# Bringing two kinds of short matmul bursts together in a Fourier and max-out kernel

## The chip, the cores and the metric

One core of a Trainium2 chip runs the whole program. The metric is device time in microseconds, the median of several executions. Less is better.

## The reference

```
X = np.fft.rfft(x, axis=1)                 # x: 8 batches of 3072 x 256
Yr = Xr @ w_r - Xi @ w_i + b_r
Yi = Xr @ w_i + Xi @ w_r + b_i
Y = soft_threshold(Yr, 0.01) + 1j * soft_threshold(Yi, 0.01)
y = np.fft.irfft(Y, n=3072, axis=1)        # then 24576 tokens of 256
h = max(y @ w1, y @ w2, y @ w3)            # 256 x 768 each
out = h @ w_out                            # 768 x 256
```

## The kernel before

**The Fourier part** of a batch is cut into stages. 3072 is 96 times 32. `stage_a` (L615) transforms over the 96 for one *quad*, four of the 32 columns, so a batch has eight quads i = 0 to 7. `stage_b` (L779) does the transform over the 32 for one of twelve groups k, `stage_w`, `stage_w1` and `stage_w2` multiply by the complex weights, `finish_w` (L905) splits the thresholded result *v* into a high and a low half-precision part, and `stage_q` (L934) is the first half of the inverse. `inverse` (L1077) is its second half. Between stages the data goes through device memory: a_d after stage a, z_d after stage q.

**Two of the stages use quarter-array matmuls.** From batch 3 on, `stage_a` multiplies 48 rows by 64 columns (L625), and `stage_q` for the middle groups multiplies *v* as 64 by 64 (L960). Each is a *burst* of 12 matmuls that run four at a time, three rounds of 512 columns, and fills two PSUM tiles. `stage_q` handles two groups in one burst, at k = 1, 3, 5, 7, 9, and group 10 alone in a burst of 256 columns. All other matmuls use the full array.

**The max-out part** is the main loop. It goes over batches b, eight chunks c of a batch and six slices f of the 768, 48 *slots* a batch. A slot has the first product of a new tile pu (six matmuls of 384 columns, `up` with i = 0, then a Relu in place on ScalarE), the second product of the tile before (`up` with i = 1, then h, on VectorE for every third f, else on ScalarE), and `down`, nine matmuls or more of 256 columns into pd. Everything is done in high and low halves, so each product is three matmuls (`mm3`, L184 to L186), and each result is split: ScalarE writes hi (hh, vb, xhl, tt), VectorE writes lo.

**The order around the change** is set by a list of events. `at(position, function, index)` puts a stage call at a position counted in slots, and `run_until` (L1006) runs what is due three times in a slot: after the first product, between the second product and `down`, and after `down`. So the Fourier work of batch b + 1 is threaded between the products of batch b, and stage a of batch b + 2 beside it. Group k of batch b has its base at `(b - 1) * SLOTS - 1.2 + 2.72 * (k + 2)` (L994), and its calls stand at offsets from it; quad i of batch b has its base at `(b - 2) * SLOTS + 5.6 * i` (L980).

**PSUM** has eight tiles of 512 columns. After the start, `ff_tile` gives tiles of one ring of three, "ff", to every Fourier stage (px, py, pi, pa, pz, pt). The ring "up" of three holds the pu tiles, and the ring "dn" of two holds pd. A new tile of a ring waits until the third tile before it (the second, in "dn") has been read for the last time. Both tiles of a stage-a burst come from "ff" before the change. Engines take their instructions strictly in the order written, so an instruction that waits holds up all that stand behind it on its engine.

Of the kernel before, what the change touches and what calls it, by code (L numbers as in the profile page):

```python
# [9 lines left out]
F32 = mybir.dt.float32  # L10
# [91 lines left out]
def fourier_maxout_kernel(  # L102
# [3 lines left out]
    NB, S, D = x.shape  # L106
    FF = w1.shape[1]
    P = 128
# [6 lines left out]
    NJP = 12  # L115
    SLOTS = NCH * NF
    NATIVE = 2 * NCH
    HALF_X = 3 * NCH
    SEVEN = {NB - 1: range(NF)}
    EARLY = NCH + 5  # L120
    FIRST = 32

    const = ctx.enter_context(tc.tile_pool(name="const", bufs=1))
# [3 lines left out]
    ps = ctx.enter_context(tc.tile_pool(name="ps", bufs=3, space=PSUM))  # L127
# [36 lines left out]
    def in_turn(turn=True):  # L164
        both = ExitStack()
        if turn and "slot" in st:
            for e in ("act", "dve"):
              if e in st:
                both.enter_context(tc.issue_after(st[e].ins))
        return both  # L170
# [12 lines left out]
    def mm3(o, lh, ll, rh, rl, start=True, stop=True, **kw):  # L183
        nc.tensor.matmul(o, lh, rh, start=start, stop=False, **kw)  # L184
        nc.tensor.matmul(o, lh, rl, start=False, stop=False, **kw)  # L185
        st["mm"] = nc.tensor.matmul(o, ll, rh, start=False, stop=stop, **kw)  # L186
# [4 lines left out]
    def ff_tile(name):  # L191
        tag = spare[0]
        if len(spare) > 1:
            spare.append(spare.pop(0))
        return ps.tile([P, 512], F32, name=name, tag=tag, bufs=2 if tag == "dn" else 3)
# [28 lines left out]
    def raw_tile(name):  # L224
        return ffn.tile([P, 1536], F32, name=name, tag="raw", bufs=8)

    def quad_tile(name):
        return fft.tile([P, NQ * D], F32, name=name, bufs=1 if name == "zq" else 2)[0:96]
# [259 lines left out]
    def at(pos, fn, i, k=None, n=None):  # L488
        if n is None or 0 <= k < n:
            events.append((pos, len(events), fn, i))  # L490

    def batch(b, kind):
        if (b, kind) not in st:
            if kind in "az":
                st[b, kind] = dram.tile([96, N2, D], F32, name=kind + "_d")
            else:
                w = 2 * NCH if kind == "x" else 2 * NJP
                st[b, kind] = fft.tile([P, w], F32, name="mx" + kind, bufs=3)
        return st[b, kind]
# [9 lines left out]
    def load_x(q):  # L509
        b, q4 = divmod(q, NCH)  # L510
        xv = x[b].rearrange("(n1 n2) d -> n1 n2 d", n2=N2)[:, q4 * NQ:(q4 + 1) * NQ, :]
        with tc.issue_after(st["ld"].ins) if q >= EARLY else nullcontext():
            if q == EARLY - 1:
                pairs = [fft.tile([P, 2, D], F32, name="xv", tag="vl", bufs=3)[0:N1] for _ in range(2)]
# [3 lines left out]
                return  # L518
            if 2 <= q < NCH or NCH + 2 <= q < EARLY:
                xq = raw_tile("xr")[0:N1, 0:NQ * D]  # L520
# [17 lines left out]
    def largest_x(q, i, xp):  # L538
        b, q4 = divmod(q, NCH)
        with tc.issue_after(quiet[0]) if q < EARLY else in_turn():  # L540
            nc.vector.tensor_reduce(
                out=batch(b, "x")[0:N1, 2 * q4 + i:2 * q4 + i + 1], in_=xp, axis=AX.X,
                op=ALU.max, apply_absolute_value=True,
            )
# [36 lines left out]
    def split_x(q):  # L581
# [12 lines left out]
        for i, xp in enumerate(pairs):  # L594
            if q >= EARLY:
                largest_x(q, i, xp)
# [11 lines left out]
    def store_a(q, r):  # L608
        b, q4 = divmod(q, NCH)
        nc.gpsimd.dma_start(  # L610
            out=batch(b, "a")[r, q4 * NQ:(q4 + 1) * NQ, :],
            in_=st["aq", q][r].rearrange("p (n d) -> p n d", n=NQ),
        )

    def stage_a(q):  # L615
        b, q4 = divmod(q, NCH)
        if q >= HALF_X:
            xt = st.pop(("xs", q))
            pa = [ff_tile("pa") for _ in range(2)]
            aq = fft.tile([P, NQ * D], F32, name="aq", bufs=2)  # L620
            for t, i in ((0, 0), (0, 1), (1, 0)):
                for r in range(2):
                    rows = slice(64 * r, 64 * r + 48)
                    for h in range(2):
                        st["mm"] = nc.tensor.matmul(  # L625
                            pa[r][64 * h:64 * h + 64], ft[rows, t], xt[rows, i, h],
                            start=t == i, stop=t == 1,
                        )
            av = batch(b, "a").rearrange("(k e c) n d -> e k c (n d)", e=2, c=2)
            for r in range(2):  # L630
                o = aq[:, 512 * r:512 * r + 512]
                nc.scalar.activation(out=o, in_=pa[r], func=AF.Copy, scale=1.0 / (X_SCALE * F_SCALE))  # L632
                for h in range(2):
                    n = q4 * NQ * D + h * 512
                    nc.gpsimd.dma_start(out=av[1 - r, :, :, n:n + 512], in_=o[64 * h:64 * h + 48])  # L635
            return
        st["aq", q] = aq = first_quads[q] if q < EARLY else quad_tile("aq")
        for i, xp in enumerate(st.pop(("xs", q))):
          with tc.issue_after(st["gate"]) if EARLY <= q < NATIVE else nullcontext():
            pa = ff_tile("pa")  # L640
            if q < NATIVE:
                nc.tensor.matmul(pa[0:96], fr, xp, start=True, stop=True)  # L642
            else:
                mm3(pa[0:96], fh, fl, *xp)
            nc.scalar.activation(
                out=aq[:, i * 512:i * 512 + 512], in_=pa[0:96], func=AF.Copy
            )
        if NCH <= q < EARLY:
            behind_z.append((q4, aq))
            return  # L650
        store_a(q, slice(0, 96 if b else FIRST))
        if NCH <= q < HALF_X and q4 == NCH - 1:
            scale_x(b, 2 * NCH)

    def scale_x(b, n, and_then=None):
        low, add = st["lim", "x"]

        def scales(e):
            st[b, "sx"] = power("s0x", e, -1.0, 261.0), power("s1x", e, 1.0, add)
            m = small("mv", bufs=2)  # L660
            nc.vector.tensor_scalar(
                out=m, in0=e, scalar1=add, scalar2=st["eb"], op0=ALU.add, op1=ALU.max
            )
            nc.vector.tensor_scalar(out=m, in0=m, scalar1=230.0, scalar2=None, op0=ALU.min)
            st[b, "sv"] = power("s0v", m, -1.0, 231.0), power("s1v", m, 1.0, 11.0)
            nc.vector.tensor_scalar(
                out=st[b, "sv"][1], in0=st[b, "sv"][1], scalar1=-1.0, scalar2=None, op0=ALU.mult
            )
            if and_then:
                and_then()  # L670

        exponent_of(st.pop((b, "x"))[0:N1, 0:n], "x", 23, 0xFF, low, scales)
# [261 lines left out]
    def stage_q(k):  # L934
# [35 lines left out]
        if kb == NJP - 1:  # L970
# [4 lines left out]

            exponent_of(st.pop((b, "u")), "u", 23, 0xFF, low, scales)

    for q in range(EARLY, NB * NCH):
        b, i = divmod(q, NCH)
        p = i if b == 1 else 9 + 5.2 * i if b == 2 else (b - 2) * SLOTS + 5.6 * i  # L980
        at(p - (3 if b == 1 else 5 if b == 2 else 8), load_x, q)
        if q >= HALF_X:
            at(p - 1, sum_x, q)
        at(p - 0.4 * (q >= HALF_X), split_x, q)
        at(p + 1, stage_a, q)
        if q >= HALF_X:
            p = 9 + 5 * i if b == 3 else (b - 3) * SLOTS + 5.5 * i + 5
            at(p - 4, load_m, q)
            at(p, largest_m, q)
            if i == NCH - 1:  # L990
                at(p + 1, scale_m, b)
    for b in range(1, NB):
        for k in range(-2, NJP + 1):
            p = 8 + 2.13 * (k + 2) if b == 1 else (b - 1) * SLOTS - (1.2 if b > 2 else 0.4) + 2.72 * (k + 2)  # L994
            for d, fn, i in (
                (0, load_a, k + 3), (-2.2 if b > 2 else -1.6, split_a, k + 1), (1.6, finish_w, k - 1),
                (1, stage_b, k + 1), (4 if k < NJP else 3, stage_q, k - 1), (2, stage_w, k), (2.4, stage_w2, k),
            ):
                at(p + d, fn, b * NJP + i, i, NJP)
            if k == -2:  # L1000
                at(p - (2.5 if b > 2 else 0), load_a, b * NJP)
# [292 lines left out]
    def idle_matmuls(n):  # L1294
        p = ff_tile("idle")
        for _ in range(n):
            nc.tensor.matmul(p, zeros[:, 0:P], zeros, start=True, stop=True)
# [8 lines left out]
    for q in range(NCH):  # L1306
        split_x(q)
        stage_a(q)
    for q in range(NCH):
        store_a(q, slice(FIRST, 96))  # L1310
    idle_matmuls(26)
# [89 lines left out]
    for q in range(NCH, EARLY):  # L1401
        split_x(q)
        if q < EARLY - 1:
            stage_a(q)
# [127 lines left out]
```

## Time and profile before

| | us |
|---|---|
| median of 3 runs | 1742.68 (1740.84 to 1744.57) |
| the profiled execution's own time | 1737.65 |
| its span, first to last instruction | 1735.9 |
| TensorE matmul busy | 1713.4, 99% of the span |
| VectorE busy | 1269.0, 73% |
| ScalarE busy | 1169.1, 67% |
| GpSimd busy | 292.2, 17% |
| granted TensorE clock | full speed in all 40 slices of the span |

Matmul durations in the trace overlap, since a matmul starts before the one ahead of it has ended. What one costs in a stream is read from the distance between starts.

### The profile page before, as it was taken

Reading aid. Unit: us, or ns where it says so; the run is one execution under the profiler, and the core shown is the slowest. Engines: PE = TensorE matmul, PEld = TensorE weight load, DVE = VectorE, ACT = ScalarE, POOL = GpSimd, SP = SyncE. Lnnn points to the kernel's source line nnn. Section 1 sums busy time; section 2 is a strip of 40 time slices with the busy share of each in tenths; the row PEclk is TensorE's granted clock in tenths of the full one; section 3 lists DMA queues with packets and bytes.
Section 4 is the critical chain, followed back from the end, with each engine's and each line's share of the span. In section 5 each row is a group of like instructions: output and inputs, shape, how many; then the busy total and the mean of one; then the engine's idle time right before and its main releaser. Section 6 shows DMA issues by size and latency. Waiting matters only on the chain.

```text
span 1735.9 us, 42087 instructions
## 1 busy us (share of the span) xinstructions
PE 1713.4 (99%) x16171; PEld 1278.0 (74%) x16171; DVE 1269.0 (73%) x2690; ACT 1169.1 (67%) x2493; POOL 292.2 (17%) x523
## 2 busy tenths in 40 slices
PE   8999999999999999999999999999999999999998
PEld 5866777677776777777777777777777777778998
DVE  2887887687866788678876688757787467667775
ACT  4567676677766777667775777667776566666775
POOL 2101012111221212211221111211222110110000
PEclk9999999999999999999999999999999999999999
DMA  9866565577646767466766567555753443422121
GB/s 294 249 183 195 161 167 162 159 183 190 186 120 178 181 185 192 133 175 177 191 168 167 156 178 204 159 143 153 191 160 106 121 126 104 122 78 64 56 60 34
DMA packets 203863, 269.61 MB, mean 155 GB/s; under 512 B 31438, under 2 KB 153262, under 8 KB 203566
## 3 DMA queue, kind: packets, MB, share of 16 engines
q1 hardware_dynamic: 171294, 193.34, 42.4%
q0 software_dynamic: 24736, 66.62, 12.0%
q10 hardware_dynamic: 7632, 6.95, 1.4%
q8 instruction: 128, 2.10, 0.5%
q14 instruction: 73, 0.60, 0.1%
HBM read 124.31 MB, written 75.50 MB: 115 GB/s over the span
## 4 chain that ended last, share of the span: by engine, by line
PE 81%; DVE 9%; DMA 5%; ACT 4%; issue 1%; SPq 1%; ACTq 0%; POOL 0%; DVEq 0%; POOLq 0%
PE pu L184 11%; PE pu L186 11%; PE pu L185 11%; PE pd L184 8%; PE pd L186 8%; PE pd L185 8%; PE py L184 3%; PE py L186 3%; PE py L185 3%; PE pi L1091 2%; PE px L792 2%; PE pa L625 2%; PE pz L960 2%; PE pu L1176 2%; PE pa L642 1%
## 5 line engine op out<-in xcount | busy, mean ns | idle before, releaser
L184 PE MATMUL pu<-yh,wuh 128*128 128x384 f16 x1344 | 438.6, 326 | 0.0
L186 PE MATMUL pu<-yh,wul 128*128 128x384 f16 x1344 | 438.0, 326 | 0.0
L185 PE MATMUL pu<-yl,wuh 128*128 128x384 f16 x1344 | 438.0, 326 | 0.0
L184 PE MATMUL pd<-woh,hh 128*128 128x256 f16 x1152 | 314.1, 273 | 0.6 <-ACT o L1273 0.4
L186 PE MATMUL pd<-woh,hh 128*128 128x256 f16 x1152 | 313.8, 273 | 0.1
L185 PE MATMUL pd<-wol,hh 128*128 128x256 f16 x1152 | 313.8, 273 | 0.0
L176 DVE TENSOR_TENSOR hh<-h,hh 128x384 f16<-128x384 f32 x336 | 185.9, 553 | 110.2 <-ACT hh L175 109.9
L1142 ACT ACTIVATE pu<-pu 128x384 f32<-128x384 f32 x336 | 160.7, 478 | 145.1 <-PE pu L186 135.1
L175 ACT ACTIVATE hh<-h 128x384 f16<-128x384 f32 x336 | 174.4, 519 | 70.2 <-DVE h L1146 64.9
L186 PEld LDWEIGHTS <-wul 128*128 128x128 f16 x1344 | 131.4, 98 | 86.7
L635 POOL DMA_DIRECT2D a_d<-aq x160 | 94.9, 597 | 584.9 <-ACT aq L632 573.5
L184 PEld LDWEIGHTS <-wuh 128*128 128x128 f16 x1344 | 131.3, 98 | 83.3 <-issue 21.6
L1278 POOL DMA_DIRECT2D out_dram<-o x189 | 104.5, 559 | 449.2 <-ACT o L1273 446.0
L185 PEld LDWEIGHTS <-wuh 128*128 128x128 f16 x1344 | 131.4, 98 | 62.5 <-issue 1.0
L1150 ACT ACTIVATE h<-pu 128x384 f32<-128x384 f32 x226 | 109.4, 484 | 47.1 <-PE pu L186 42.7
L184 PE MATMUL py<-wch,tt 128*128 128x256 f16 x504 | 137.4, 273 | 0.6 <-ACT aq L632 0.3
L186 PE MATMUL py<-wch,tt 128*128 128x256 f16 x504 | 137.3, 273 | 0.0
L185 PE MATMUL py<-wcl,tt 128*128 128x256 f16 x504 | 137.3, 272 | 0.0
L184 PEld LDWEIGHTS <-hh 128*128 128x128 f16 x1152 | 112.6, 98 | 33.0 <-issue 11.8
L185 PEld LDWEIGHTS <-hh 128*128 128x128 f16 x1152 | 112.7, 98 | 21.5 <-issue 0.5
L1105 DVE SCALAR_TENSOR_TENSOR y<-pi,ye 128x192 f32<-128x192 f32 x252 | 110.4, 507 | 21.8 <-ACT ye L1099 21.6
L186 PEld LDWEIGHTS <-hh 128*128 128x128 f16 x1152 | 112.6, 98 | 13.8 <-DVE hh L176 0.4
(288 smaller groups left out, 3551.0 us busy)
## 6 DMA issues: line engine op xcount, KB each, us to landing
zq<-z_d SPq DMA_DIRECT2D x63, 384.0 KB, 4.7
out_dram<-o POOLq DMA_DIRECT2D x189, 128.0 KB, 3.5
ab<-a_d SPq DMA_DIRECT2D x84, 256.0 KB, 4.3
ab<-ab SPq DMA_DIRECT2D x336, 64.0 KB, 2.8
vb<-vb SPq DMA_DIRECT2D x308, 64.0 KB, 2.9
z_d<-zs POOLq DMA_DIRECT2D x70, 256.0 KB, 3.9
xm<-in_x_dram SPq DMA_DIRECT2D x40, 384.0 KB, 4.3
a_d<-aq POOLq DMA_DIRECT2D x160, 96.0 KB, 3.3
```

What stands on the lines that cost most here:

```text
L175: nc.scalar.activation(out=hi, in_=src, func=AF.Copy)
L176: later(lambda: nc.vector.tensor_tensor(out=lo, in0=src, in1=h, op=ALU.subtract))
L184: nc.tensor.matmul(o, lh, rh, start=start, stop=False, **kw)
L185: nc.tensor.matmul(o, lh, rl, start=False, stop=False, **kw)
L186: st["mm"] = nc.tensor.matmul(o, ll, rh, start=False, stop=stop, **kw)
L625: st["mm"] = nc.tensor.matmul(pa[r][64 * h:64 * h + 64], ft[rows, t], xt[rows, i, h], start=t == i, stop=t == 1,)
L635: nc.gpsimd.dma_start(out=av[1 - r, :, :, n:n + 512], in_=o[64 * h:64 * h + 48])
L792: nc.tensor.matmul(pv[:, h, :, g // 2, g % 2], ah[:, g // 2, g % 2, h * P:(h + 1) * P], mb_sb[:, i, 4 * kb + g].rearrange("p (c m) -> p c ...
L1105: nc.vector.scalar_tensor_tensor(out=yv[:, e], in0=pv[:, 0], scalar=(1 - 2 * e) * Y_SCALE, in1=ev, op0=ALU.mult, op1=ALU.add,)
L1142: st["act"] = nc.scalar.activation(out=p, in_=p, func=AF.Relu)
L1150: st["act"] = nc.scalar.activation(out=h32, in_=p, func=AF.Relu, scale=H_SCALE)
L1278: nc.gpsimd.dma_start(out=out_v[b, c, t + i], in_=o[:, i])
```

## The change

A function `pace` holds the base of group k; for batches 3 and later it is 1.2 slots sooner than before (-2.4 in place of -1.2). With PAIR = 6.12, `stage_q` for the even k of batches 2 to 6 (those are the two-group bursts) moves from base + 4 to base + 6.12. Quads 3 to 7 of batches 3 to 7 are put at the same position, ahead of it in the list, with their loads, sums and splits 1 slot and more before. The second tile of every stage-a burst comes from the ring "up".

```diff
+    PAIR = 6.12
...
-            pa = [ff_tile("pa") for _ in range(2)]
+            pa = [ff_tile("pa"), ps.tile([P, 512], F32, name="pa", tag="up", bufs=3)]
...
+    def pace(b, k):
+        return 8 + 2.13 * (k + 2) if b == 1 else (b - 1) * SLOTS - (2.4 if b > 2 else 0.4) + 2.72 * (k + 2)
+
     for q in range(EARLY, NB * NCH):
         b, i = divmod(q, NCH)
-        p = i if b == 1 else 9 + 5.2 * i if b == 2 else (b - 2) * SLOTS + 5.6 * i
+        p = i if b == 1 else 9 + 5.2 * i if b == 2 else (b - 2) * SLOTS + 5.6 * i if i < 3 else pace(b - 1, 2 * i - 4) + PAIR - 1
...
-        at(p + 1, stage_a, q)
+        at(pace(b - 1, 2 * i - 4) + PAIR if b > 2 and i > 2 else p + 1, stage_a, q)
...
-            p = 8 + 2.13 * (k + 2) if b == 1 else (b - 1) * SLOTS - (1.2 if b > 2 else 0.4) + 2.72 * (k + 2)
+            p = pace(b, k)
...
-                (1, stage_b, k + 1), (4 if k < NJP else 3, stage_q, k - 1), (2, stage_w, k), (2.4, stage_w2, k),
+                (1, stage_b, k + 1), (PAIR if 1 < b < NB - 1 and k % 2 == 0 and k < NJP - 1 else 4 if k < NJP else 3, stage_q, k - 1), (2, stage_w, k), (2.4, stage_w2, k),
```

Line numbers after the change are higher by 1 to 4. In the rows below a number behind a tile's name tells its buffers apart.

First place: TensorE in batch 3 of the main loop, where stage a's burst for quad 4 ends. Before:

```order
L625 LDWEIGHTS zeros_72
L625 MATMUL pa_12363<-xhl_12268,zeros_72 64x512
L184 LDWEIGHTS wuh_81
L184 MATMUL pu_12385<-yh_12110,wuh_81 128x384
L185 LDWEIGHTS wuh_81
```

After:

```order
L626 LDWEIGHTS zeros_72
L626 MATMUL pa_12546<-xhl_12450,zeros_72 64x512
L961 LDWEIGHTS zeros_72
L961 MATMUL pz_12566<-vb_12002,zeros_72 64x512
L961 LDWEIGHTS zeros_72
```

The burst of stage a was followed by a full-array product; now the burst of stage q follows it with nothing between. There are 25 such places, five in each of the main loop's batches 1 to 5.

Second place: ScalarE around the last pair of batch 3 of the main loop. h32 and hh are h and its high part, aq and zs are what is read out of pa and pz. Before, around the same product of *v* (group 9):

```order
L1150 ACTIVATE h32_13706<-pu_13632 128x384
L175 ACTIVATE hh_13708<-h32_13706 128x384
L966 ACTIVATE zs_13730<-pz_13716,s1v_7532 128x512
L966 ACTIVATE zs_13733<-pz_13717,s1v_7532 128x512
L1142 ACTIVATE pu_13747<-pu_13747 128x384
L175 ACTIVATE hh_13798<-h32_13796 128x384
```

After:

```order
L176 ACTIVATE hh_13785<-h32_13783 128x384
L633 ACTIVATE aq_13790<-pa_13788 128x512
L633 ACTIVATE aq_13790<-pa_13789 128x512
L967 ACTIVATE zs_13823<-pz_13809,s1v_7532 128x512
L967 ACTIVATE zs_13826<-pz_13810,s1v_7532 128x512
L1146 ACTIVATE pu_13858<-pu_13858 128x384
L1154 ACTIVATE h32_13876<-pu_13769 128x384
L176 ACTIVATE hh_13878<-h32_13876 128x384
L967 ACTIVATE zs_13852<-pz_13838,s1v_7532 128x256
```

Two read-outs in a row have become four, and between the read-out of group 9's second tile and that of group 10's first (pz_13838) there are now three instructions, where there were nine.

Third place: VectorE at quad 2 of batch 3, one burst before the first pair. tt is the low part of what is read out of px. Before, the nearest h on VectorE:

```order
L837 TENSOR_SCALAR t_11917<-u_11914 128x512
L839 ISA u_11914,mxu_11518<-t_11917,u_11914 128x512
L839 ISA mxu_11518 128x1
L1146 TENSOR_SCALAR h32_11947<-pu_11832 128x384
L179 SCALAR_TENSOR_TENSOR vb_12050<-u_11914,s0v_7528,vb_12050 128x512
```

After:

```order
L177 TENSOR_TENSOR hh_11901<-h32_11899,hh_11901 128x384
L180 SCALAR_TENSOR_TENSOR vb_12002<-u_11864,s0v_7528,vb_12002 128x512
L180 SCALAR_TENSOR_TENSOR tt_11972<-px_11955,tt_11972 128x2x256
L1150 TENSOR_SCALAR h32_11982<-pu_11870 128x384
L809 SCALAR_TENSOR_TENSOR s_11974<-px_11955,s_11974 128x256
```

The h that frees the tile pu_11870 now stands behind the low part of a tt, which itself needs ScalarE's high part, and on ScalarE that stands behind the two read-outs of the burst.

## Rows read from the trace of the kernel before

**Rows 1.** The page: busy time, and the chain that ended last, by engine.

```profile
PE 1713.4 (99%) x16171; PEld 1278.0 (74%) x16171; DVE 1269.0 (73%) x2690; ACT 1169.1 (67%) x2493; POOL 292.2 (17%) x523
...
PE 81%; DVE 9%; DMA 5%; ACT 4%; issue 1%; SPq 1%; ACTq 0%; POOL 0%; DVEq 0%; POOLq 0%
```

**Rows 2.** Timeline (start us, us, engine, line, tiles): TensorE at two bursts.

```profile
802.46 0.27 PE L186 MATMUL py<-wch,tt 128*128 128x256 f16 x1
802.66 0.84 PE L625 MATMUL pa<-xhl,zeros 48*64 48x512 f16 x12
803.44 0.34 PE L184 MATMUL pu<-yh,wuh 128*128 128x384 f16 x1
...
920.59 0.33 PE L186 MATMUL pu<-yh,wul 128*128 128x384 f16 x1
920.85 0.52 PE L960 MATMUL pz<-vb,zeros 64*64 64x256 f16 x12
921.30 0.34 PE L184 MATMUL pu<-yh,wuh 128*128 128x384 f16 x1
```

**Rows 3.** Timeline of ScalarE behind the first burst of rows 2.

```profile
803.54 1.08 ACT L632 ACTIVATE aq<-pa 128x512 f32<-128x512 f32 x2 [1.02 <-PE pa L625]
```

**Rows 4.** VectorE and TensorE: bursts of quads 0 and 1, main batch 3.

```profile
753.63 0.74 DVE L179 SCALAR_TENSOR_TENSOR xhl<-xq,xx,xhl 112x512 f16<-112x512 f32 x1
753.92 1.13 PE L625 MATMUL pa<-xhl,zeros 48*64 48x512 f16 x12
775.82 0.41 DVE L808 SCALAR_TENSOR_TENSOR s<-px,s 128x256 f32<-128x256 f32 x1
776.05 1.01 PE L625 MATMUL pa<-xhl,zeros 48*64 48x512 f16 x12
```

**Rows 5.** Timeline of TensorE, main batch 1: two longer waits.

```profile
418.27 0.82 PE L792 MATMUL px<-mb_all,ab 128*128 128x64 f16 x16 [0.51 <-DMA ab<-ab]
...
437.49 1.20 PE L625 MATMUL pa<-xhl,zeros 48*64 48x512 f16 x12
```

**Rows 6.** Timeline of TensorE, where main batch 6 begins.

```profile
1361.87 0.38 PE L1091 MATMUL pi<-ga_sb,ze 96*128 96x48 f16 x8 [1.14 <-DMA ze<-zl]
```

**Rows 7.** TensorE and ScalarE: a second product and its read-out h.

```profile
756.78 0.33 PE L186 MATMUL pu<-yh,wul 128*128 128x384 f16 x1
757.20 0.49 ACT L1150 ACTIVATE h<-pu 128x384 f32<-128x384 f32 x1 [0.45 <-PE pu L186]
```

**Rows 8.** ScalarE by line: busy us, mean ns of one, idle before.

```profile
L175 ACT ACTIVATE hh<-h 128x384 f16<-128x384 f32 x336 | 174.4, 519 | 70.2 <-DVE h L1146 64.9
L178 ACT ACTIVATE tt<-px 128x512 f16<-128x512 f32 x84 | 49.0, 584 | 1.4 <-PE px L792 0.5
L966 ACT ACTIVATE zs<-pz,s1v 128x512 f32<-128x512 f32 (+1 forms) x84 | 50.0, 643 | 0.8 <-PE pz L960 0.5
L1273 ACT ACTIVATE o<-pd,s1u 128x512 f32<-128x512 f32 x126 | 67.2, 571 | 2.8 <-PE pd L186 2.8
L1099 ACT ACTIVATE ye<-pi 128x192 f32<-128x192 f32 x126 | 40.5, 323 | 36.8 <-PE pi L1091 36.0
```

**Rows 9.** VectorE by line, same columns.

```profile
L1146 DVE TENSOR_SCALAR h<-pu 128x384 f32<-128x384 f32 x110 | 60.7, 551 | 18.2 <-PE pu L186 18.2
L179 DVE SCALAR_TENSOR_TENSOR tt<-px,tt 128x512 f16<-128x512 f32 x84 | 57.7, 687 | 11.4 <-ACT s L805 11.0 <-issue 0.3
L1105 DVE SCALAR_TENSOR_TENSOR y<-pi,ye 128x192 f32<-128x192 f32 x252 | 110.4, 507 | 21.8 <-ACT ye L1099 21.6
```

**Rows 10.** GpSimd by line, its DMA issues.

```profile
L635 POOL DMA_DIRECT2D a_d<-aq x160 | 94.9, 597 | 584.9 <-ACT aq L632 573.5 <-issue 11.4
L969 POOL DMA_DIRECT2D z_d<-zs x70 | 51.0, 729 | 189.7 <-ACT zs L966 184.2 <-ACT cs L883 5.2 <-issue 0.2
```

**Rows 11.** Line L969: time from issue to landing.

```profile
DMA to landing us min/median/max: 1.7/3.8/7.2
```


## The prediction

> **What bounds the kernel.** I read the page first. TensorE is busy 99% of the span and holds 81% of the chain that ended last; VectorE follows with 9% [rows 1]. Matmuls stand packed, so time can go only if TensorE issues less, or loses fewer of its short waits. Next come the timelines at the bursts, for what one costs; then the groups by line, for how soon the other engines give a PSUM tile back; last the DMA issues and their landing. Everything is summed against the profiled execution's 1737.65 us, which is 5.03 below the median of 1742.68; I add 5.03 at the end. A difference of 0.2%, 3.5 us, is about what a measurement of this kernel can tell from no change.
>
> **What a burst costs.** A product of 256 columns is followed by its like 0.109 us later, one of 384 columns 0.163. Between the last product ahead of stage a's burst and the first behind it lie 803.44 - 802.46 = 0.98 us; less 0.109, the burst takes 0.87 of the stream. Group 10's, with half the columns, takes 921.30 - 920.59 - 0.163 = 0.55 [rows 2]. The 0.32 between them are the half of the columns, so 512 columns take 0.64 and 0.23 is paid per burst whatever its size. I take the 0.23 to be the change of the array's form on the way in and out. With nothing between two bursts it is paid once: 1.51 in place of 1.74. The order has 25 pairs, 25 x 0.23 = **-5.75 us**. The other end is 0: the two bursts have 48 and 64 rows, and if that alone is a change of form, the pair pays twice. I take the saving, because both have four matmuls side by side on 64 columns each.
>
> The Trainium skill ("TensorEngine Tiling (Array Packing)", Restrictions and Gotchas) says that changing the tiling mode, not just the tile, drains TensorE. By it a pair in one mode saves the 5.75 and a pair in two modes nothing; the fixed 0.23 agrees with it, but no row shows two bursts in a row.
>
> **Waits that go.** In main batches 2 to 5, quad 0's burst takes 1.13 us instead of 0.84: its low part is ready only at 753.63 + 0.74 = 754.37, behind another low part on VectorE. Quad 1's takes 1.01, because its second tile in "ff" waits for the s that ends at 775.82 + 0.41 = 776.23 [rows 4]. In the new order that other low part stands elsewhere, and the second tile comes from "up". 4 x (0.29 + 0.17) = **-1.8 us**. In main batch 1 a burst takes 1.20, 0.36 too long, and a px waits 0.51 for a load [rows 5]; the order is rearranged at both. Both may go or stay, 0 to -0.87; I take **-0.4**.
>
> The inverse's wait for ze, 1.14 us where main batch 6 begins [rows 6], has eight such loads in one queue ahead of it at unchanged positions. I cost it at nothing. If the 1.2 slots by which the batches come sooner moved it, half of it at each of six batch starts would give or cost 3.4, counted in the range.
>
> **Waits that come.** After the pairing four tiles are filled within 1.5 us and ScalarE reads all of them. The read-out of a single burst begins 803.54 - 802.57 = 0.97 us after the last product's end and takes 1.08 for two tiles [rows 3]. I followed the new order by hand at every pair and its neighbours. A second product's end is followed by its h 0.26 us later (757.20 - 756.78 - 0.163), and that takes 0.49 [rows 7]. So a tile is free about 0.8 us after its last product. The ring "up" now leaves one `down` (0.98 us) between last use and reuse at the narrow places, enough if nothing stands in a queue. At pairs 1 to 4 of main batches 2 to 5, and at quads 0 and 1, I find nothing that does. Four kinds of place remain:
>
> - *Main batch 1, pairs 3 and 4.* A pi stands right ahead of the pair, and the burst of *v* takes over its tile 0.87 us later. Reading pi takes ScalarE's 0.32 (ye) and VectorE's two of 0.51 [rows 8, 9], plus 0.26 to begin: 1.6. That is at least 0.73 each; with what is queued ahead of them 1.3 and 1.8. Bounds 1.5 to 3.6, I take **+2.6**.
> - *Quad 2.* Counted from the last product ahead, the two aq end at 0.97 + 1.08 = 2.05, tt at 2.63, its low part at 3.32, and h, now behind that, at 3.87 [rows 3, 8, 9]. TensorE wants the tile at 3.30 (burst 0.87, px 0.47, product 0.98, `down` 0.98). 0.6 in main batches 3 to 5, 0.2 in batch 2: **+2.0**, bounds 0 and 2.7.
> - *Group 10's burst behind the fifth pair.* Its second half takes the tile of the pair's first pz. h is done on VectorE at 0.26 + 0.55 = 0.81, hh on ScalarE at 1.33, two aq at 2.4, the first zs at 3.05 [rows 8, 9]. TensorE is there at 1.51 + 0.98 and a tenth, 2.6. 0.5 in four batches: **+2.0**, bounds 0 and 2.6.
> - *The store behind it.* zs has two buffers, and group 10's zs waits on ScalarE until the pair's zs have landed in memory. GpSimd first issues four a_d from about 1.9 on, at 0.60 each, then z_d at 0.73 each [rows 10]: the first z_d begins at 4.3 and lands, after a median of 3.8 [rows 11], at 8.1. Behind the waiting zs stands o2 (0.57 [rows 8]), which frees the pd tile that TensorE wants at about 8.45: zs of half the columns about 0.45 (between 0.32 and 0.64 [rows 8]) and o2 0.57 make 9.1, so 0.7, and with the second half's zs and o some 0.8 late in all. With a landing of 3.0 or less nothing is late. Median and nothing are about as near, since the record goes from 1.7 to 7.2; I take half, 0.4 in four batches, **+1.6**, bounds 0 and 17 (0.8 + 3.4 each).
>
> **Sum.** -5.75 - 1.8 - 0.4 + 2.6 + 2.0 + 2.0 + 1.6 = +0.25: 1737.65 + 0.25 + 5.03 = 1742.9, said as **1743**.
>
> The Trainium skill ("TensorEngine Tiling (Array Packing)", PSUM Bottleneck) warns that tiling speeds TensorE but not the reading of PSUM, so that the copy may become the bottleneck. A pair of 1.51 us against four read-outs of 1.08 + 1.29 is such a case, and it is what speaks against this change.
>
> **The rivals.**
>
> *Faster: ScalarE and VectorE absorb it.* The last three waits add up from queue positions, each 0.4 to 0.8 us on engines that are busy 67% and 73% [rows 1]. If those engines run a little ahead of my count, as the 70 us of idle time in front of hh suggest [rows 8], the three vanish and the first keeps its lower bound: -5.75 - 1.8 - 0.4 + 1.7 = -6.3, 1736.4 us. Against it: the same products stand behind one another four times, so a miscount of a tenth either way hits all four.
>
> *Slower: the store holds ScalarE.* Place: behind the fifth pair, main batches 1 to 5. It decides when z_d takes over about 3.0 us from issue to landing; the median is above that. At 5.5, midway from median to longest, each place costs 0.8 + 1.7 = 2.5, five cost 12.5 in place of the 1.6: +11.2, 1754; at 4.5 it is 1.5 each, 7.5, +6.2, 1749. For it: six transfers now leave GpSimd in a row where two or four did. Against: a store from a tile already read out lands in 1.7 at best, so half of the record may be quick enough.
>
> *No pairing gain.* If 48 and 64 rows are two forms, the 5.75 stay: +6.0, 1749.
>
> **How the numbers follow.** My forecast, saving and new waits within 3.5 us of each other, gets 0.38; faster 0.36, since the saving rests on two measured rows and the new waits on counts along queues; the store 0.20; no pairing gain 0.06. The likeliest case alone spans 1739.5 to 1746.5. The range leaves out the lower end of "faster" with the ze wait gone too, and the long landings: **1735 to 1750.5**. Faster by over 0.2%: 0.36; within: 0.38; slower: 0.26.
>
> **What would show it.** Pairing right: the distance over a pair, from the product ahead to the first behind, is 1.51 and no read-out is late in it; wrong: 1.74. The quad bursts 0 and 1 take 0.84. At quad 2, the product two behind shows a wait on VectorE's h of 0.6; at the burst of group 10 one on ScalarE's zs of 0.5; at the next group's pd one on ScalarE's o, with zs in front of it waiting for z_d. If none of these three shows, the rival to the fast side holds. If TensorE's sum of waits falls or rises elsewhere, above all at the batch starts, my list of places was wrong.

## The result, and the profile after

The changed kernel takes 1762.85 us (median of 5, 1760.71 to 1765.26), the kernel before 1742.68: a ratio of 1.0115, 95% interval 1.0098 to 1.0131. It is slower by some 20 us, where no change was forecast; the range ended at 1750.5. Since the kernel before moved between 1740 and 1744 us from one set of runs to the next, experiments are compared by their ratio to it.

The page of the changed kernel, busy time and the chain by engine:

```profile
PE 1718.4 (97%) x16171; PEld 1285.0 (73%) x16171; DVE 1270.1 (72%) x2690; ACT 1172.1 (66%) x2493; POOL 290.5 (16%) x523
...
PE 58%; DVE 19%; ACT 10%; DMA 7%; issue 4%; SPq 1%; POOL 0%; ACTq 0%; DVEq 0%; POOLq 0%
```

Against [rows 1] TensorE's share of the chain fell from 81% to 58%, VectorE's rose from 9% to 19% and ScalarE's from 4% to 10%: TensorE now waits, and what it waits for stands on those two.

The distance between the bursts of quad 0 gives each main batch its length (timeline of TensorE, changed kernel):

```profile
557.55 0.84 PE L626 MATMUL pa<-xhl,zeros 48*64 48x512 f16 x12
...
770.98 0.84 PE L626 MATMUL pa<-xhl,zeros 48*64 48x512 f16 x12
...
981.84 0.84 PE L626 MATMUL pa<-xhl,zeros 48*64 48x512 f16 x12
...
1192.82 0.84 PE L626 MATMUL pa<-xhl,zeros 48*64 48x512 f16 x12
```

The same starts in the kernel before are 547.04, 753.92 [rows 4], 961.09 and 1167.36, and the first such burst stands at 337.09 before and 339.15 after. The last column is the best version found, below.

| stretch | before | after | experiment 9 |
|---|---|---|---|
| up to the first burst of quad 0 | 337.1 | 339.2 | 339.4 |
| main batch 1 | 209.9 | 218.4 | 209.9 |
| main batch 2 | 206.9 | 213.4 | 206.4 |
| main batch 3 | 207.2 | 210.9 | 205.8 |
| main batch 4 | 206.3 | 211.0 | 206.3 |
| from there to the end of the span | 568.5 | 570.6 | 570.7 |

These are single profiled executions (spans 1735.9, 1763.4 and 1738.5). The first two lie 27.5 us apart, the medians 20.2: the profiled execution of the kernel before was 5.0 below its median, that of the changed kernel 2.4 above. So the table shows where the time is lost, and its sizes are somewhat too large. Main batches 2 to 5, which are built alike, are called regular below. The loss is 8.5 us in main batch 1 and 4 to 7 in each of main batches 2 to 4; main batch 5, which shows no wait behind pairs 3 and 5, is in the last row.

The quad bursts show 0.84 where [rows 4] had 1.13. A pair, from the product ahead to the first behind (timeline of TensorE, main batch 3, first pair):

```profile
829.40 0.33 PE L187 MATMUL pu<-yh,wul 128*128 128x384 f16 x1
829.65 0.84 PE L626 MATMUL pa<-xhl,zeros 48*64 48x512 f16 x12
830.32 0.82 PE L961 MATMUL pz<-vb,zeros 64*64 64x512 f16 x12
831.08 0.28 PE L185 MATMUL pd<-woh,hh 128*128 128x256 f16 x1
```

831.08 - 829.40 - 0.163 = 1.52 us. The pairing does what it should: 1.74 - 1.52 = 0.22 saved, 5.5 us over 25 pairs.

What takes it back, in the same batch, is seen in the waits of TensorE (start us, us, engine, line, operation; the idle time and its releaser in brackets):

```profile
833.36 0.56 PE L1095 MATMUL pi<-ga_sb,ze 96*128 96x48 f16 x16 [0.48 <-ACT aq L633]
...
834.43 0.63 PE L793 MATMUL px<-mb_all,ab 128*128 128x64 f16 x16 [0.51 <-ACT zs L967]
...
887.77 0.27 PE L185 MATMUL pd<-woh,hh 128*128 128x256 f16 x1 [1.24 <-ACT o L1277]
...
911.10 0.63 PE L793 MATMUL px<-mb_all,ab 128*128 128x64 f16 x16 [0.71 <-ACT aq L633]
...
944.03 0.27 PE L185 MATMUL pd<-woh,hh 128*128 128x256 f16 x1 [0.95 <-ACT o L1277]
```

They stand behind pairs 1, 1, 3, 4 and 5. The brackets leave out some 0.15 us of each gap (the fourth begins 911.10 - 910.07 - 0.163 = 0.87 us late, not 0.71), so they cost about 4.6; with 0.4 in group 10's burst and 0.2 behind quad 1, less some 1.6 saved, that is about the 3.7 by which the batch is longer. Each is a read-out that came late on ScalarE.

*At the first pair* ScalarE's timeline reads:

```profile
830.80 0.72 ACT L179 ACTIVATE vb<-u,s0v 128x512 f16<-128x512 f32 x1 [1.54 <-DVE mxu L840]
831.42 0.47 ACT L1154 ACTIVATE h<-pu 128x384 f32<-128x384 f32 x1
831.80 0.62 ACT L695 ACTIVATE ab<-ab 128x512 f16<-128x512 f32 x1
832.32 0.51 ACT L176 ACTIVATE hh<-h 128x384 f16<-128x384 f32 x1
832.73 1.07 ACT L633 ACTIVATE aq<-pa 128x512 f32<-128x512 f32 x2
833.68 1.28 ACT L967 ACTIVATE zs<-pz,s1v 128x512 f32<-128x512 f32 x2
```

vb, the high half of the next group's *v*, waits 1.54 us for VectorE's soft threshold, of which mxu is the last step. Behind it stand h, ab and hh, and only then the four read-outs. The burst of stage a began at 829.65, and its first read-out at 832.73, 3.1 us later; in [rows 2, 3] it was 803.54 - 802.66 = 0.9.

*At the third pair* vb, behind the two aq, waits for the same mxu, and zs and o stand behind it:

```profile
885.26 0.72 ACT L179 ACTIVATE vb<-u,s0v 128x512 f16<-128x512 f32 x1 [1.54 <-DVE mxu L840]
885.89 1.25 ACT L967 ACTIVATE zs<-pz,s1v 128x512 f32<-128x512 f32 x2
887.03 1.05 ACT L1277 ACTIVATE o<-pd,s1u 128x512 f32<-128x512 f32 x2
```

*At the fourth* an hh waits 2.82 us for an h that VectorE takes up only behind some of the same threshold steps, and vb (0.72) stands between it and aq, which begins at 910.47, 2.7 us after the burst at 907.74. *At the fifth* it is the store:

```profile
942.93 0.47 ACT L967 ACTIVATE zs<-pz,s1v 128x256 f32<-128x256 f32 x1 [1.64 <-DMA z_d<-zs]
943.30 0.68 ACT L1277 ACTIVATE o<-pd,s1u 128x512 f32<-128x512 f32 x1
```

By line, ScalarE's idle time in front of zs went from 0.8 [rows 8] to 11.6 us, 10.2 of it for z_d:

```profile
L967 ACT ACTIVATE zs<-pz,s1v 128x512 f32<-128x512 f32 (+1 forms) x84 | 50.7, 654 | 11.6 <-DMA z_d<-zs 10.2 <-PE pz L961 1.5
```

*In main batch 1* the two pairs behind a pi wait inside the burst of *v* for VectorE to read that pi:

```profile
462.12 0.93 PE L961 MATMUL pz<-vb,zeros 64*64 64x512 f16 x10 [2.10 <-DVE y L1109]
...
490.24 1.06 PE L961 MATMUL pz<-vb,zeros 64*64 64x512 f16 x8 [1.70 <-DVE y L1109]
```

### The profile page after: what moved, and what is told of

It reads as the page before. It is cut to its first block, busy times and chain, and to the rows that moved or that the text cites. A ratio compares the mean times of both kernels' runs of the same rounds, so it can differ in the third digit from the quotient of the medians.

```text
span 1763.4 us, 42035 instructions
## 1 busy us (share of the span) xinstructions
PE 1718.4 (97%) x16171; PEld 1285.0 (73%) x16171; DVE 1270.1 (72%) x2690; ACT 1172.1 (66%) x2493; POOL 290.5 (16%) x523
## 4 chain that ended last, share of the span: by engine, by line
PE 58%; DVE 19%; ACT 10%; DMA 7%; issue 4%; SPq 1%; POOL 0%; ACTq 0%; DVEq 0%; POOLq 0%
PE pu L185 8%; PE pu L187 8%; PE pu L186 8%; PE pd L185 6%; PE pd L187 6%; PE pd L186 6%; PE py L185 2%; PE py L187 2%; PE py L186 2%; PE pi L1095 2%; DVE y L1109 2%; DVE zl L180 2%; DMA z_d<-zs 2%; PE px L793 2%; DVE hh L177 1%
## 5 line engine op out<-in xcount | busy, mean ns | idle before, releaser
L185 PEld LDWEIGHTS <-hh 128*128 128x128 f16 x1152 | 112.7, 98 | 32.8 <-issue 11.9
```

## The experiments

**Theory.** An instruction of ScalarE that waits for something else stands ahead of the pair's read-outs, and TensorE needs those tiles soon: vb at pairs 1 and 3, the store behind pair 5. In main batch 1 it is the burst of *v* itself that waits, for VectorE's reading of pi. **Rivals:** four read-outs in a row are too much for ScalarE whatever stands ahead; the ring "up" has become too narrow; the sooner groups do it.

### 1: vb behind the read-outs

```diff
-            split_later(v[:, 0], v[:, 1], u, st[b, "sv"][0])
+            with tc.issue_after(st["read"].ins) if "read" in st else nullcontext():
+                split_later(v[:, 0], v[:, 1], u, st[b, "sv"][0])
...
-                nc.scalar.activation(out=zs[:, 0:n], in_=pz[q], func=AF.Copy, scale=st[b, "sv"][1])
+                st["read"] = nc.scalar.activation(out=zs[:, 0:n], in_=pz[q], func=AF.Copy, scale=st[b, "sv"][1])
```

> Edit: on ScalarE each vb is issued behind the last zs read-out written before it, so that no vb, which waits for VectorE's maximum, stands ahead of a pair's four read-outs. Theory (a waiting vb holds the read-outs): the late pi and px behind the first pair (1.23 us together) and the late pd behind the third (1.40) go in main batches 2 to 5, some -9 us, about 1754. Rival (four read-outs in a row are too many by themselves): the same waits stay, -2 to 0, 1761 to 1763.

Measured: 1751.74 us, ratio 1.0047 (1.0030 to 1.0064) against 1.0115: 0.68% of the kernel, 11.9 us, where some 9 were expected. At the same pair (ScalarE, main batch 3):

```profile
821.48 0.49 ACT L1155 ACTIVATE h<-pu 128x384 f32<-128x384 f32 x1 [0.50 <-PE pu L187]
821.87 0.62 ACT L695 ACTIVATE ab<-ab 128x512 f16<-128x512 f32 x1
822.38 0.51 ACT L176 ACTIVATE hh<-h 128x384 f16<-128x384 f32 x1
822.80 1.07 ACT L633 ACTIVATE aq<-pa 128x512 f32<-128x512 f32 x2
823.75 1.28 ACT L968 ACTIVATE zs<-pz,s1v 128x512 f32<-128x512 f32 x2
824.89 0.75 ACT L179 ACTIVATE vb<-u,s0v 128x512 f16<-128x512 f32 x1
```

The stage-a burst begins at 821.37; aq follows 1.4 us later, the four read-outs stand in a row as before, and pi, px and the pd behind pair 3 show no wait. The late px behind pair 4 is gone as well: its hh still waits (2.64 us), but with vb out of the way aq begins at 898.46, 1.7 us after the burst at 896.76, soon enough. So the row of four read-outs is not what costs: it holds up TensorE only when it starts late. Behind the fifth pair the wait grew:

```profile
932.26 0.47 ACT L968 ACTIVATE zs<-pz,s1v 128x256 f32<-128x256 f32 x1 [3.00 <-DMA z_d<-zs]
```

TensorE came there sooner, the store no sooner; pd now began 2.31 us late by its bracket, 0.95 in the changed kernel, and in the 4 us from 934 on the granted clock was 0.60 of full speed. So main batch 3 as a whole gained only 0.7 us (972.84 - 762.71 = 210.1), and main batch 2 gained 3.4.

### 2: no pairs in main batch 1

Lines of this diff, and of later ones, are cut to the part that differs.

```diff
-5.6 * i if i < 3 else pace(b - 1, 2 * i - 4) + PAIR - 1
+5.6 * i if i < 3 or b == 3 else pace(b - 1, 2 * i - 4) + PAIR - 1
...
-+ PAIR if b > 2 and i > 2 else p + 1, stage_a, q)
++ PAIR if b > 3 and i > 2 else p + 1, stage_a, q)
...
-(PAIR if 1 < b < NB - 1
+(PAIR if 2 < b < NB - 1
```

> Edit: main batch 1 keeps its single bursts, pairs stay in main batches 2 to 5. Theory (the pair's burst of v takes over the tile of a pi just ahead): the waits 0.45, 2.10 and 1.70 us inside the bursts go, and so do the half-speed stretches behind two of them; 5 x 0.22 of pairing is given back: -5 to -8 us, 1755 to 1758. Rival (main batch 1 waits whatever is paired): -1 to +1, 1762 to 1764.

Measured: 1756.26, ratio 1.0075 (1.0058 to 1.0092), 0.40% or 7.0 us less than the changed kernel, and main batch 1 takes 550.37 - 338.26 = 212.1 where it took 218.4. The theory's number holds. The waits alone are 0.45 + 2.10 + 1.70 = 4.3; most of the rest is the clock, below.

### 3: a tile of its own for group 10's first zs

```diff
-                zs = fft.tile([P, 2, D], F32, name="zs")
+                zs = fft.tile([P, 1, D], F32, name="zt", bufs=1) if n == 1 and q == 0 else fft.tile([P, 2, D], F32, name="zs")
```

> Edit: the first zs of group 10 has a tile of its own, so that it needs not wait until the pair's zs are stored. Theory (the store holds ScalarE, and o behind it): the late pd behind the fifth pair, 1.0 to 2.5 us in four batches, 5.6 in all, goes but for what the second zs still waits: -3 to -5, 1758 to 1760. Rival (o is late for the read-outs ahead of it): within 1 of 1763.

Measured: 1761.95, ratio 1.0106 (1.0089 to 1.0124): no difference that counts. It is a miss of the edit rather than of the theory, as ScalarE's timeline shows:

```profile
934.94 0.47 ACT L967 ACTIVATE zt<-pz,s1v 128x256 f32<-128x256 f32 x1
...
939.96 0.47 ACT L967 ACTIVATE zs<-pz,s1v 128x256 f32<-128x256 f32 x1 [1.83 <-DMA z_d<-zs]
940.33 0.68 ACT L1277 ACTIVATE o<-pd,s1u 128x512 f32<-128x512 f32 x1
```

The first zs no longer waits, but the second was put in its place ahead of o and waits for the same store.

### 4: the ring "ff" for both tiles of stage a

```diff
-            pa = [ff_tile("pa"), ps.tile([P, 512], F32, name="pa", tag="up", bufs=3)]
+            pa = [ff_tile("pa") for _ in range(2)]
```

> Edit: both tiles of a stage-a burst come from the ring ff again, pairs stay. Theory (the ring up is not what costs): a pair then needs four tiles of a ring of three, its last waits for the first aq, about 0.9 us for each of 25 pairs and 0.17 for each quad 1: +15 to +23, 1778 to 1786. Rival (narrow places of the ring up cost the time): faster than 1763 by 3 or more.

Measured: 1797.03, ratio 1.0298 (1.0276 to 1.0321). The fourth tile of a pair takes the place of the first and waits inside the burst for aq, up to 1.88 us. That is 1.8% or 32 us more than the changed kernel, above the 15 to 23 expected: I had put 0.9 us on each pair, and the profile shows up to twice that, since aq itself is late; behind most of these waits the granted clock fell besides (0.50 of full speed from 842 to 846, behind a wait of 1.80). The ring "up" is what makes the pair possible, not what spoils it.

### 5 and 6: groups 10 and 11 later, with the vb rule; then without main batch 1's pairs

```diff
-k < NJP - 1 else 4 if k < NJP else 3, stage_q, k - 1)
+k < NJP - 1 else 5.2 if 2 < b < NB - 1 and k == NJP - 1 else 4 if k < NJP else 4.2 if 2 < b < NB - 1 else 3, stage_q, k - 1)
```

> Edit: the vb rule of the first experiment, and in main batches 2 to 5 the bursts of groups 10 and 11 later (5.2 and 4.2 slots after their bases in place of 4 and 3), so that group 10's zs comes some 1.8 slots behind the fifth pair. Theory (the store of the pair's zs holds ScalarE, the zs of group 10 standing ahead of o): the late pd there, 2.56, 2.47 and 1.89 us in the first experiment's profile, goes: -5 to -7 on 1751.7, 1745 to 1747. Rival (the wait only moves to group 11's zs or to the inverse): -2 to +2, 1750 to 1754.

> Edit: as the run before it, and no pairs in main batch 1. If the three causes (vb ahead of the read-outs, pi's tile in main batch 1, the store behind the fifth pair) stand apart, their gains add up: 1762.85 - 11.1 - 6.6 - 6 = 1739, below the kernel before by 3 to 5. Rival (they share one wait, and removing one removes part of the next): 1743 to 1747.

Measured: 1743.05, ratio 1.0014 (1.0004 to 1.0024), and 1741.61, ratio 1.0006 (0.9997 to 1.0016). On the 1742.68 of the first comparison these ratios are 1745.1 and 1743.7 us. Later groups give 0.33% on top of experiment 1, 5.8 us, as the theory said: zs is out of o's way. ScalarE still waits there for z_d, but behind o instead of ahead of it (experiment 5, main batch 3):

```profile
927.36 1.04 ACT L1278 ACTIVATE o<-pd,s1u 128x512 f32<-128x512 f32 x2
931.30 1.09 ACT L968 ACTIVATE zs<-pz,s1v 128x256 f32<-128x256 f32 x2 [2.52 <-DMA z_d<-zs]
```

Group 10's burst, which no longer takes the pair's tile, lasts 0.52 in the timeline as before the change, 0.93 in the changed kernel; that is part of the gain.

Experiment 6 shows that gains did not simply add up. Leaving out main batch 1's pairs gave 0.08%, which the intervals don't tell from nothing, instead of 0.40%; the time is the rival's. Main batches 2 to 4 took 205.7 to 206.3 us, but main batch 1 took 555.40 - 340.54 = 214.9, more than in experiment 2. Whether the rule for vb costs there is what experiment 9 asks.

### 7 and 8: one part of the change alone on the kernel before

```diff
-- (1.2 if b > 2 else 0.4) + 2.72 * (k + 2)
+- (2.4 if b > 2 else 0.4) + 2.72 * (k + 2)
```

> Edit: the kernel before, with only the bases of batches 3 and later 1.2 slots sooner. Theory (the loss comes from the pairs): within 2 of 1743. Rival (the shift by itself puts vb or the splits in front of what TensorE waits for): slower by 4 or more.

> Edit: the kernel before, with only the second tile of every stage-a burst from the ring up. Theory (the ring up is not what costs): quad 1's 0.17 goes in four batches, and about 1 more with it: 1741 to 1743. Rival (a narrow ring up costs by itself): slower by 3 or more.

(Experiment 8 has the line of the change's diff with the ring "up", and nothing else.) Measured: 1772.07, ratio 1.0185 (1.0167 to 1.0203), and 1739.55, ratio 0.9994 (0.9985 to 1.0004). The ring alone is worth nothing either way. The sooner groups alone cost more than the whole change, against my expectation. Without the quads moved along, bursts of *v* and of stage a come close behind one another by chance, both on the ring "ff", and the same vb stands ahead of zs (ScalarE, then TensorE, main batch 3):

```profile
869.87 0.72 ACT L178 ACTIVATE vb<-u,s0v 128x512 f16<-128x512 f32 x1 [2.54 <-DVE mxu L839]
...
873.05 0.68 ACT L966 ACTIVATE zs<-pz,s1v 128x512 f32<-128x512 f32 x1
```

```profile
873.78 1.38 PE L625 MATMUL pa<-xhl,zeros 48*64 48x512 f16 x12 [2.50 <-ACT zs L966]
```

Such a wait of TensorE for zs stands once in each of main batches 2 to 5 (2.52, 2.50, 2.50 and 1.73 us). It says that bursts standing badly against vb and the threshold cost time without any pair. It doesn't say what the shift costs in the changed kernel; experiment 11 does.

### 9: the remedies in main batches 2 to 5 only

Experiment 6 with the rule for vb made conditional on b > 2; main batch 1 carries the groups of b = 2.

> Edit: the three remedies in main batches 2 to 5 only (vb behind the read-outs, groups 10 and 11 later, no pairs in main batch 1), main batch 1 without the vb rule. Theory (in the run before with the rule everywhere main batches 2 to 4 took 205.7 to 206.3 us where the kernel before took 206.3 to 207.2, and main batch 1 gave 4.9 back): main batch 1 returns to within 2 of the 210 it took before, and the whole is 0.1 to 0.3% faster than the kernel before. Rival (main batch 1 loses by the new ring or the sooner groups): within 0.1% of it.

Measured: 1737.91, ratio 0.9977 (0.9968 to 0.9986). This version is 0.23% faster than the kernel before. Main batch 1 is back at 209.9 us, so the rule for vb did cost there; main batch 3 takes 1.4 us less than before, and main batches 2 and 4 give 0.5 and nothing: at the starts of the batches the inverse's wait for ze is longer than before in places (0.86 at main batch 5).

What the rule does in main batch 1 can be read from experiment 6 (ScalarE, VectorE, TensorE):

```profile
463.34 0.72 ACT L179 ACTIVATE vb<-u,s0v 128x512 f16<-128x512 f32 x1 [3.76 <-DMA vb<-vb]
464.10 0.75 DVE L180 SCALAR_TENSOR_TENSOR vb<-u,s0v,vb 128x512 f16<-128x512 f32 x1 [2.50 <-ACT vb L179]
470.59 0.32 PE L185 MATMUL pu<-yh,wuh 128*128 128x384 f16 x1 [1.49 <-ACT h L1155]
```

Two groups use one tile for vb in turn, and the first is moved out of it by DMA. Held back until behind a read-out, the first vb came only 8.1 us ahead of the second (455.22 and 463.34; 12.1 in experiment 9), so the second waited for the move, and both engines stood. TensorE's waits in main batch 1 add up by their brackets to 7.1 us in experiment 6 and 2.8 in experiment 9: 4.3 of the 5.0 us between them.

### 10: groups 10 and 11 later, alone

> Edit: the changed kernel with groups 10 and 11 later, without the vb rule. Theory (two separate causes): only the waits behind the fifth pair go, 1.0 to 2.5 us in four batches, -4 to -6 on 1762.85: 1757 to 1759. Rival (the store's wait shows only once vb is out of the way): 0 to -2, 1761 to 1763.

Measured: 1756.10, ratio 1.0083 (1.0063 to 1.0104), 0.32% or 5.6 us less than the changed kernel, nearly what the same edit gave in experiment 5; the ends of the two intervals just overlap (the changed kernel's begins at 1.0098). In the trace no pd waits behind the fifth pair any more, with vb where it was: the store is a cause by itself, apart from vb. The 5.6 are not the store's alone. Group 10's burst is back at 934.75 - 934.04 - 0.163 = 0.55 from 0.95, some 1.6 us in four batches, so about 4.0 are left for the store.

### 11: the change without its shift

```diff
-- (2.4 if b > 2 else 0.4) + 2.72 * (k + 2)
+- (1.2 if b > 2 else 0.4) + 2.72 * (k + 2)
```

> Edit: the changed kernel with the bases of batches 3 and later back where they were, the pairs still 6.12 behind them. Theory (where the pair stands against its own groups' vb decides, and that is kept): 1758 to 1768. Rival (the 1.2 slots by which the batches come sooner are the cause): 1745 or less.

Measured: 1754.31, ratio 1.0078 (1.0064 to 1.0092): below the theory's range and far above the rival's. Leaving out the shift gives back 0.37%, 6.4 of the 20 us, so it is not the cause by itself, but it isn't neutral. The premise that the pair keeps its place against vb was wrong: in main batch 3 vb waits 0.15 us at the third pair instead of 1.54, and at the first not at all. But without the shift the pairs meet the inverse elsewhere, and the second and third pair of each regular batch now wait for a pi's tile, as in main batch 1 (TensorE, main batch 3, third pair):

```profile
881.95 0.83 PE L961 MATMUL pz<-vb,zeros 64*64 64x512 f16 x10 [1.09 <-DVE y L1109]
```

The shift trades this wait for the ones at vb.

## Why the prediction was wrong

Step by step, in the prediction's own order:

- **Pairing, -5.75.** Right: 0.22 per pair, -5.5. 48 and 64 rows are no two forms; the rival of no pairing gain is out. By the Trainium skill's rule ("TensorEngine Tiling (Array Packing)", Key Properties under Tiling Modes, not the section that the prediction names) a change of mode, not just of tile, drains TensorE. The 1.52 agrees with one mode.
- **Waits that go, -1.8 and -0.4.** Quads 0 and 1 show 0.84, so they went; the product behind quad 1 gained a new gap of 0.2. In main batch 1 the px still waits for its load.
- **Pairs 1 to 4, "I find nothing that does" stand in a queue.** This is the step that failed. Their waits make up 3.5 of the 5.3 us that main batch 3 loses before savings, and the rule for vb took 11.9 us away. I followed the new order on each engine and gave every instruction ahead of a read-out its duration, but took it to be ready when its turn came. For vb I did not go on to VectorE, where reading, adding, the threshold and its maximum have to end first. ScalarE's groups by line would have asked for it. Here is vb before, and then after:

```profile
L178 ACT ACTIVATE vb<-u,s0v 128x512 f16<-128x512 f32 x84 | 60.5, 720 | 53.8 <-DVE mxu L839 48.5 <-DMA vb<-vb 4.2
```

```profile
L179 ACT ACTIVATE vb<-u,s0v 128x512 f16<-128x512 f32 x84 | 60.4, 720 | 53.0 <-DVE mxu L840 49.7 <-DMA ab<-a_d 1.5 <-DMA vb<-vb 1.1
```

  The idle time is the same, some 49 us for mxu. It cost TensorE next to nothing before, because what stood behind vb was not urgent; the change put read-outs there.
- **Main batch 1, +2.6 (bounds 1.5 to 3.6).** Right mechanism, size too small: leaving these pairs out gave 7.0. The waits were 2.10 and 1.70 where I had 1.3 and 1.8, pair 2 waited 0.45 as well, and the half-speed stretches behind them were not in my sum.
- **Quad 2, +2.0.** Wrong: TensorE shows no wait there in any main batch from 2 to 5.
- **Group 10's burst, +2.0.** Right: it takes 938.02 - 936.96 - 0.109 = 0.95 where 0.55 stood in [rows 2], 0.4 in each of four batches.
- **The store, +1.6 (half of 0.8 in four batches).** Right mechanism, too small: moving groups 10 and 11 away gave 5.6 to 5.8, some 4.0 of it the store's. In main batch 3 z_d was issued at 939.09 and zs began at 942.93, 3.84 us, about the median landing; pd was 1.1 us late where the full price was 0.8. Taking half of the price because some landings are shorter was the first error. The second shows in main batch 2: pd waited twice (1.24 and 0.90) and the clock fell behind it, which had no place in the sum. Main batch 5 shows no such wait.
- **The rivals.** The slower one, the store, is a cause, but only about a fifth of the loss. It named the right pattern, a waiting instruction on ScalarE ahead of o, at one of the four kinds of place where it happens.

The warning of the Trainium skill ("TensorEngine Tiling (Array Packing)", PSUM Bottleneck), that reading PSUM may become the limit, was not what happened: with vb behind them, the four read-outs of pairs 1 to 4 cost TensorE nothing in main batch 3.

It was not tried to keep the pairs of main batch 1 with another place for their pi. Nor is each wait priced by itself: the remedies overlap (experiment 6), and the vb rule's 11.9 us cover waits in main batches 1 to 5.

## What to carry to other kernels

When two bursts are put side by side, look for what stands ahead of their read-outs on the reading engine and waits for a third engine: it costs nothing where it stood alone, and it holds up everything behind it once four tiles hang on it. In tracing an order by hand, ask of each instruction in a queue when its inputs are there, not only how long it takes. A ring of two that is emptied by a store needs the landing time, here about 3.8 us behind the issue, between its users.

## What the hardware showed that was not expected

A wait of about 2 us on TensorE could cost more than its length. In main batch 1 of the changed kernel the granted clock was at full speed up to the wait at pair 3 and fell behind it, and again at pair 4 (TensorE by stretch: us, busy, granted clock, DMA share, GB/s):

```profile
455.00:459.00 4.00, 4.00 (x62) 1.00 0.85 206
459.00:462.00 3.00, 0.96 (x14) 1.00 0.79 145
462.00:466.00 4.00, 3.88 (x25) 0.59 0.55 142
466.00:487.00 21.00, 21.00 (x188) 1.00 0.45 122
487.00:490.00 3.00, 1.54 (x32) 1.00 0.93 253
490.00:494.00 4.00, 3.77 (x33) 0.57 0.83 232
494.00:500.00 6.00, 6.00 (x64) 1.00 0.22 77
```

The engine idled 2.10 and 1.70 us, and in the 4 us behind each the granted clock was on average 0.59 and 0.57 of full speed, so for the most part the lower of its levels, 1.2 GHz instead of 2.4. Those stretches held 2.4 and 2.3 us of full-speed work, so each wait cost another 1.6 to 1.7 us: 3.3 for both, which with the waits' 4.3, less the 1.1 of pairing given back, accounts for 6.5 of the 7.0 us that experiment 2 measured. Main batch 2, which lost 6.5 us where main batches 3 and 4 lost 3.7 and 4.7, has a third such place, at the waits 1.24 and 0.90 behind its fifth pair:

```profile
732.00:736.00 4.00, 3.69 (x32) 0.57 0.35 124
```

Not every such wait is followed by a fall. In the changed kernel the clock stayed at full speed behind 1.70 us for ze at 1389.25, in experiment 3 behind 2.28 at 730.16, and in experiment 7 behind 2.52 at 661.32, although behind the like wait of 2.50 at 873.78 it was 0.64 from 874 to 878. What decides between them stays open here.
